# Column transforms moved between the last channels' products, and a PSUM tile for each step of the last channel, in a spectral block with a feed-forward network on one Trainium2 core

## The chip, the cores and the metric

The kernel runs on one core of one Trainium2 chip. The metric is the time of one execution in microseconds (us) on the device; smaller is better. A core has a matrix engine (PE, or TensorE), a vector engine (DVE), a scalar engine (ACT), a general engine (POOL), and queues that issue DMA transfers (here SP's). Every engine runs its own instructions strictly in the order in which they were written; an instruction that needs another engine's result waits for a semaphore, and everything behind it on its engine waits too.

## The reference

```python
def _A_ref(x, w_r, w_i):                     # spectral mixing, S = 2048 rows, D = 576 columns
    X = rfft2(x.astype(float32), axes=(-2, -1))
    X = X * (w_r + 1j * w_i)
    return irfft2(X, s=(S, D), axes=(-2, -1)).astype(bfloat16)

def _B_ref(x, w_gate, w_up, w_down):         # D = 576, F = 4608
    return (_gelu(x @ w_gate) * (x @ w_up)) @ w_down

h = x + _A_ref(_layernorm(x), A_w_r, A_w_i)
h2 = h + _B_ref(_layernorm(h), B_w_gate, B_w_up, B_w_down)
```

x has 1 x 2048 x 576 values in bfloat16; the spectral weights have 2048 x 289, the feed-forward weights 576 x 4608 (twice) and 4608 x 576.

## The kernel before, in words

The whole first half, up to `h`, is a chain of small matrix products; the second half is the feed-forward network, four chunks of 512 rows.

**The spectral half.** The transform over the 2048 rows is split into 16 by 128. After the forward products the work runs over eight "channels" k, in the order `[1, 2, 3, 4, 5, 6, 7, 0]`, so the last channel is k = 0 and the one before it k = 7. The main loop is a pipeline written out by hand: in step i it issues

- `f2` (L449), the forward column transform of one channel: six products into a PSUM tile, and one copy to SBUF by ACT (L464) that makes the tile `pq`;
- `f3(k, half)` (L474), four products (L471 and L472) from `pq[k]` and `pq[k+8]` into a PSUM tile `gh_ps`, and a cast by ACT. For the ordinary channels the casts make `g` and `hs` (L492). For k = 0 they make `xab` directly (L483), and the first two of the four products need only `pq[0]`, the others `pq[8]`;
- `wmul` (L504), the multiplication with the spectral weights on DVE (L519 to L531), which writes the tile `Zt`. For the last channel it is done in two parts of columns, so `Zt` becomes ready in two halves;
- `i3(k, s)` (L535), the inverse products of channel k in three steps s. Each step writes a PSUM tile `eo_ps` that ACT, or DVE in one case, copies into `EO[x]`. An ordinary channel has ten products (L547 and L549). The last channel has eight products (L570) in each of its three steps. In the kernel before, steps 0 and 1 of every channel share one PSUM tile; for the last channel the copy of step 0 (ACT, L578) reads the tile's first half and that of step 1 (DVE, L578) its second half. Step 2 is copied by ACT at L583, and for ordinary channels at L556, steps 0 and 1 together at L551.

`EO[0]` is complete after channel 4, `EO[1]` only after the last channel.

**Column transforms.** `inv_cols(x, g)` (L591) is the inverse column transform number g, 0 to 7, of half x, 0 or 1: six products (L596) into a PSUM tile `cs_ps`, and a copy out by ACT. For g = 0 and 1 these are two copies into `cs` (L619; for half 1 the second of the two goes to DVE, L617), for larger g one copy into `cw` (L609). In the kernel before, transforms (0,0), (0,1), (0,2) stand between the products of channels 6 and 7, then come channel 7, the last channel, transform (0,3), and, after the weight pools have been set up, (1,0) and (1,1).

**Row products and the head of the feed-forward.** `add_rows(0)` and `add_rows(1)` (L708, tile `y_ps`) finish the rows of blocks h = 0 to 3. DVE adds them to `h_sb` (`add_sum`, L753), ACT sums the squares (L757), and `head_rstd` makes the statistics. Blocks 0 and 1 are normalised by DVE (`norm2`, L733, tile `hrow`) and turned by a DMA transpose on SP's queue (`flip`, L745); blocks 2 and 3 are normalised into `hflat` (L141) and turned by PE (`turn`, L778), copied by ACT and DVE (L779). In between, PE does the transforms that are left: (0,4) to (0,7) and (1,2) to (1,6), and (1,7) behind the turns. The feed-forward's first product (L845) needs all four blocks in `Bt`.

**The feed-forward.** For each chunk of 512 rows, 36 blocks of 18 products (L845), a Gelu on ACT (L853) and a product on DVE (L854), then the products with `w_down` (L865). Two thirds of `w_down` are loaded by `load_wd` (L673) on SP's queue; the first of these loads goes into memory that the spectral tiles free, so it waits for the last channel's products.

**What sets the order.** The schedule is manual: instructions stand on each engine in the order of the calls. From the middle of the kernel all PSUM tiles come from one pool of four buffers (`two`, two banks each). A new tile takes the buffer whose former tile was finished with longest ago in the written order, and its first product waits for the copy that read that former tile.

Of the kernel before, what the change touches and what calls it, by code (L numbers as in the profile page):

```python
# [20 lines left out]
P = 128  # L21
# [11 lines left out]
NJT = 3  # L33
# [8 lines left out]
def kernel_body(  # L42
# [24 lines left out]
    def two(name):  # L67
        return psum.tile([P, 2, 512], FP32, name=name, tag="two", bufs=3)
# [312 lines left out]
    def twiddles():  # L381
        sine_rows()
        A.activation(TF[:, :, 1, :], ab[:], ACT.Sin, bias=nhpib[:], scale=2.0 * PI / S)
        nc.sync.dma_start(
            TI[:].rearrange("p k r q -> p (k r) q"), TF[:].rearrange("p k r q -> p (k r q)"), transpose=True
        )
        nc.sync.dma_start(wd_a[:], wd_view[:, 0:NWA, :])

    def sine_rows():


        for dst, src in (
            (DI[64:128, :, 1, :], DT[0:64, 0, :, 1, :]),
            (DS[0:64, 0, :, :], DT[64:128, 0, :, 1, :]),
            (DS[64:128, 0, :, :], DT[0:64, 1, :, 1, :]),
            (DS[0:64, 1, :, :], DT[64:128, 1, :, 1, :]),
            (DS[64:128, 1, :, :], D3[0:64, :, 1, :]),
        ):
            nc.sync.dma_start(dst, src)
# [43 lines left out]
    order = [1, 2, 3, 4, 5, 6, 7, 0]  # L443
# [5 lines left out]
    def f2(c):  # L449
        ps = two("pq_ps")  # L450
        if c == 1:
            fill(ps[:, 0, :], 4)
        col = slice(slot[c] * P, (slot[c] + 1) * P)
        for par in range(2):
            for t in (par, par + 2, 4):
                T.matmul(  # L456
                    ps[:, par, 0:JP],
                    lhsT=Bt[:, t, col],
                    rhs=DT[:, t // 2, par] if t < 4 else DF[:, par],
                    start=(t == par),  # L460
                    stop=(t == 4),
                )
        sb = wk.tile([P, 2, JP], BF16, name="pq", tag="pq", bufs=6)
        (V.tensor_copy if c == 9 else A.copy)(  # L464
            sb[:].rearrange("p r (j a) -> p r j a", a=2),
            ps[:, :, 0:JP].rearrange("p a (r j) -> p r j a", r=2),
        )
        pq[c] = sb
# [29 lines left out]
    def sums_of(k):  # L498
        g, hs = gk[k], hk[k]
        x = xab[k] = wk.tile([P, 2, 2, JP], BF16, name="xab", tag="xab", bufs=2)  # L500
        V.tensor_tensor(x[:, 0, :, 0:J], g[:, :, 0:J], hs[:, :, 0:J], ALU.subtract)  # L501
        V.tensor_tensor(x[:, 1, ::-1, 0:J], g[:, :, 0:J], hs[:, :, 0:J], ALU.add)  # L502
# [32 lines left out]
    def i3(k, s):  # L535


        x, i = place[k]
        z = zt[k][:].rearrange("p c j -> p (c j)")
        if s != 1:  # L540
            eo[k] = two("eo_ps")
        ps = eo[k]
        if k:
            pv = ps[:].rearrange("p a (n h e l) -> p (a n) e h l", n=2, h=H, l=8)
            for n, w in (((0, 0), (1, 1)), ((2, 3), (3, 4)), ((0, 2),))[s]:
                o = w * P
                T.matmul(pv[:, n], lhsT=z[:, o : o + P], rhs=TI[:, k, 1:3, :], start=True, stop=False)  # L547
                o += 2 * ZS
                T.matmul(pv[:, n], lhsT=z[:, o : o + P], rhs=TI[:, k, 0:2, :], start=False, stop=True)  # L549
            if s == 1:  # L550
                A.copy(  # L551
                    EO[x][:, 0:4, :, :, i, :].rearrange("p w h e l -> p w (h e) l"),
                    ps[:].rearrange("p a (n r l) -> p (a n) r l", n=2, l=8),
                )
            elif s == 2:
                A.copy(  # L556
                    EO[x][:, 4, :, :, i, :].rearrange("p h e l -> p (h e) l"),
                    ps[:, 0, 0 : 2 * P].rearrange("p (r l) -> p r l", l=8),
                )
            return  # L560

        pv = ps[:].rearrange("p a (n h b l) -> p (a n) b h l", n=2, h=H, l=8)
        for n, c, j, p0, m in (
            ((0, 0, 0, 0, P), (1, 0, P, 0, P)),
            ((2, 1, 64, 0, P), (3, 1, 192, 0, P)),
            ((0, 0, 256, 0, 64), (0, 1, 0, 64, 64)),
        )[s]:
            for b in range(2):
                for a in range(2):
                    T.matmul(  # L570
                        pv[p0 : p0 + m, n, b],
                        lhsT=z[:, (2 * a + b) * ZS + j : (2 * a + b) * ZS + j + m],
                        rhs=TI[:, 8 * b, 1 - a + c, :],
                        start=(a == 0),
                        stop=(a == 1),
                    )
        if s < 2:
            (V.tensor_copy if s else A.copy)(  # L578
                EO[x][:, 2 * s : 2 * s + 2, :, :, i, :].rearrange("p w h e l -> p w (h e) l"),
                ps[:, s].rearrange("p (n r l) -> p n r l", n=2, l=8),  # L580
            )
        else:
            A.copy(  # L583
                EO[x][:, 4, :, :, i, :].rearrange("p h e l -> p (h e) l"),
                ps[:, 0, 0 : 2 * P].rearrange("p (r l) -> p r l", l=8),
            )
# [4 lines left out]
    def inv_cols(x, g):  # L591

        ps = two("cs_ps")
        for e in range(2):
            for jt in range(NJT):
                T.matmul(  # L596
                    ps[:, e, 0:JP],
                    lhsT=EO[x][:, 2 * e + jt if jt < 2 else 4, 2 * g : 2 * g + 2].rearrange("p h e k l -> p (h e k l)"),
                    rhs=DI[:, :, e, :] if jt == 2 else DS[:, jt] if e else DT[:, jt, :, 0, :],
                    start=(jt == 0),  # L600
                    stop=(jt == NJT - 1),
                )
        pv = ps[:, :, 0:JP].rearrange("p t (q a) -> p t q a", q=2)
        if g >= 2:
            if x == 0 or g == 2:
                cw[x, g] = eop.tile([P, 2, JP], FP32, name=f"cw{x}{g}")[:]
            else:
                cw[x, g] = cwb[:, g - 3]
            A.activation(  # L609
                cw[x, g].rearrange("p t (a q) -> p t q a", q=2), pv, ACT.Copy, scale=Y_SCALE  # L610
            )
            return
        ts = [eop.tile([P, JP], BF16, name=f"cs{x}{g}{t}") for t in range(2)]
        for t in range(2):
            dst = ts[t][:].rearrange("p (a q) -> p q a", q=2)
            if x == 1 and t == 1:
                V.tensor_scalar(dst, pv[:, t], Y_SCALE, None, op0=ALU.mult)  # L617
            else:
                A.activation(dst, pv[:, t], ACT.Copy, scale=Y_SCALE)  # L619
        cs[x, g] = ts  # L620
# [3 lines left out]
    n = len(order)  # L624
    for i in range(n + 1):
        last = i >= n
        if not last:
            f2(order[i])
        if i == 0:
            twiddles()  # L630
        if 1 <= i <= n:
            f3(order[i - 1], 0)
        if i >= 3 and not last:
            i3(order[i - 3], 0)
        if 1 <= i <= n:
            f3(order[i - 1], 1)
            if i == 1:
                sums_of(order[0])
            else:
                wmul(order[i - 2], i - 1, order[i - 1])  # L640
        if i >= 3 and not last:
            i3(order[i - 3], 1)
        if not last:
            f2(order[i] + 8)
        if i == 0:
            weights()
        if i >= 3:
            for jt in range(0 if last else 2, NJT):
                i3(order[i - 3], jt)
        if last:  # L650
            wmul(order[i - 1], i)
        if i == 1:
            late_tables()
            scr_pool.__exit__(None, None, None)
            eop = ctx.enter_context(tc.tile_pool(name="eop", bufs=1, side="right"))
            EO = [eop.tile([P, 5, H, 2, 4, 8], BF16, name=f"EO{x}", tag=f"EO{x}") for x in range(2)]
    for g in range(3):
        inv_cols(0, g)
    for k in order[6:]:
        for jt in range(NJT):  # L660
            i3(k, jt)
    inv_cols(0, 3)

    spw.__exit__(None, None, None)
    spec.__exit__(None, None, None)
# [118 lines left out]
    def norm_row(h):  # L784
        hrow = ln2[h] = roll.tile([P, D], BF16, name="hflat", tag="hrow", bufs=4)
        normalise(V, hrow[:], mv2, rstd2, h)
# [4 lines left out]
    y1 = add_rows(1)  # L791
    add_sum(0, y0)
    add_sum(1, y0)
    inv_cols(0, 4)
    add_sum(2, y1)
    head_rstd(0)
    add_sum(3, y1)
    head_rstd(1)
    inv_cols(0, 5)
    norm2(0)  # L800
    flip(0)
    head_rstd(2)
    inv_cols(0, 6)
    head_rstd(3)
    norm2(1)
    flip(1)
    inv_cols(0, 7)
    inv_cols(1, 2)
    norm_row(2)
    norm_row(3)  # L810
    for g in range(3, 7):
# [20 lines left out]
    for tcnk in range(4):  # L832
        for gi in range(NG):
            fa = gi * FQ
            w = groups.pop(0)
            n = tcnk * NG + gi + 2
# [21 lines left out]
        for st in range(4):  # L858
            h = tcnk * 4 + st
            last = h == H - 1  # L860
# [70 lines left out]
```

## Time and profile before

| | |
|---|---|
| median of 3 runs | 510.33 us (510.31 to 510.36) |
| profiled execution, its own time | 510.62 us |
| span of the profiled execution | 508.4 us |
| PE busy | 494.4 us (97%) |
| PE weight loads busy | 287.0 us (56%) |
| DVE busy | 214.7 us (42%) |
| ACT busy | 152.4 us (30%) |
| granted PE clock | 1.0 |
| feed-forward's first product | at 79.8 us of the span |

The span runs from the first to the last instruction; the execution's own time is 2.2 us longer. Products on PE overlap: a row of the timeline gives the start and the length of one, and the next may start before it ends. In the timeline a bracket at the end of a row is the idle time of that engine before it, and the engine, tile and line that ended it. In the chain of waits each row is a piece of the chain that ended last, with its start and length. The waits are inferred from semaphore events.

### The profile page before, as it was taken

The page shows a single profiled execution, that of the slowest core. Times are in us where ns is not written, and L with a number is a line of the kernel's source. Part 1 is how long each engine was busy: PE and PEld are TensorE (multiplying, and loading weights), DVE is VectorE, ACT ScalarE, POOL GpSimd, SP SyncE. Part 2 cuts the span into 40 slices and gives each one's busy share as a digit, 9 for nine tenths or more (in the row PEclk, how much of TensorE's full clock was granted, in tenths as well). Part 3 has the DMA queues.
Part 4 walks back from the last instruction along what each step waited for, and adds up shares of the span by engine and source line. Part 5 has one row for each costly group of instructions (what it writes and reads, how often), then busy time and mean ns, then how long its engine had stood idle before and what let it go on. Part 6 is the DMA issues. An engine that isn't in the chain of part 4 may idle for free.

```text
span 508.4 us, 9921 instructions
## 1 busy us (share of the span) xinstructions
PE 494.4 (97%) x4353; PEld 287.0 (56%) x4355; DVE 214.7 (42%) x418; ACT 152.4 (30%) x265; POOL 32.6 (6%) x81
## 2 busy tenths in 40 slices
PE   6889999999999999999999999999999999999997
PEld 2457765444447774444467744444578544444775
DVE  8979964689662015433311034433201233333001
ACT  7688975233220003323210023232200132323000
POOL 8700010111110000000000000000000000000000
PEclk9999999999999999999999999999999999999999
DMA  8985057779970009998730089978500487770000
GB/s 285 230 151 154 1 153 203 148 145 198 198 148 3 0 24 206 184 202 157 143 69 0 1 175 198 189 158 159 104 0 1 115 161 159 160 153 3 13 12 25
DMA packets 86811, 60.85 MB, mean 120 GB/s; under 512 B 22640, under 2 KB 85488, under 8 KB 86768
## 3 DMA queue, kind: packets, MB, share of 16 engines
q1 hardware_dynamic: 86480, 59.03, 57.8%
q0 software_dynamic: 288, 1.18, 0.9%
q8 instruction: 34, 0.56, 0.5%
q14 instruction: 9, 0.07, 0.1%
HBM read 52.65 MB, written 2.36 MB: 108 GB/s over the span
## 4 chain that ended last, share of the span: by engine, by line
PE 90%; DVE 7%; ACT 1%; DMA 1%; issue 0%; POOL 0%; DVEq 0%; ACTq 0%
PE gu L845 55%; PE acc L865 28%; DVE m L519 2%; PE cs_ps L596 2%; PE f2t L261 2%; PE y_ps L708 1%; DVE za L525 1%; DMA h_sb<-in_A_x_dram 1%; PE f2t L249 1%; DVE xab L502 1%; PE f L270 1%; DVE Zt L530 1%; DVE zb L526 1%; DVE Zt L531 1%; DVE xab L501 0%
## 5 line engine op out<-in xcount | busy, mean ns | idle before, releaser
L845 PE MATMUL gu<-Bt,wgu 64*128 64x512 bf16 x2592 | 281.4, 376 | 0.0
L845 PEld LDWEIGHTS <-wgu 64*128 64x128 bf16 x2592 | 125.8, 94 | 152.5 <-issue 0.7
L853 ACT ACTIVATE g_sb<-gu 128x512 f32<-128x512 f32 x144 | 86.0, 597 | 301.9 <-PE gu L845 301.8
L854 DVE TENSOR_TENSOR P_sb<-g_sb,gu 128x512 bf16<-128x512 f32 x144 | 98.7, 685 | 151.8 <-ACT g_sb L853 151.8
L865 PEld LDWEIGHTS <-P_sb 128*128 128x128 bf16 x1152 | 112.4, 98 | 30.6 <-issue 2.4
L865 PE MATMUL acc<-wd,P_sb 128*128 128x288 bf16 x768 | 99.3, 286 | 0.0
L877 DVE TENSOR_TENSOR h_sb<-h_sb,acc 128x576 bf16<-128x576 bf16 x15 | 11.3, 754 | 118.2 <-PE acc L865 118.2
L865 PE MATMUL acc<-wd_a,P_sb 128*128 128x288 bf16 x384 | 52.3, 286 | 0.5 <-DVE h_sb L873 0.5
L249 PE MATMUL f2t<-h_sb,ident 128*128 128x512 bf16 x39 | 11.9, 434 | 4.4 <-DMA h_sb<-in_A_x_dram 4.4
L456 PE MATMUL pq_ps<-DT,Bt 128*128 128x290 bf16 x64 | 12.4, 287 | 0.0
L733 DVE TENSOR_SCALAR hrow<-h_sb,mv,rstd 128x1152 bf16<-128x1152 bf16 x14 | 12.1, 867 | 0.0
L138 POOL TENSOR_TENSOR rstd<-rstd,mhalf 128x1 f32<-128x1 f32 (+2 forms) x17 | 11.8, 693 | 1.4
L249 PEld LDWEIGHTS <-ident 128*128 128x128 bf16 x45 | 4.8, 107 | 11.5 <-issue 5.2
L261 PE MATMUL f2t<-F,xn 128*128 128x256 bf16 x64 | 9.7, 274 | 1.6 <-DVE xn L141 1.5
L137 POOL TENSOR_SCALAR rstd<-mv 128x1 f32<-128x1 f32 (+2 forms) x17 | 4.0, 237 | 110.1 <-DVE mv L122 109.9
L596 PEld LDWEIGHTS <-EO 128*128 128x128 bf16 x96 | 9.0, 96 | 3.0 <-issue 0.2
L456 PEld LDWEIGHTS <-Bt 128*128 128x128 bf16 x96 | 9.2, 97 | 2.5
L464 ACT CAST pq<-pq_ps 128x580 bf16<-128x580 f32 x15 | 9.9, 662 | 0.9 <-PE pq_ps L456 0.8
L120 DVE BATCH_NORM_STATS2 st<-h_sb 128x6 f32<-128x288 bf16 x22 | 9.8, 444 | 0.0
L121 DVE BATCH_NORM_STATS2 st<-h_sb 128x6 f32<-128x288 bf16 x22 | 9.7, 442 | 0.0
L471 PE MATMUL gh_ps<-pq,TF 128*128 128x289 bf16 x32 | 8.6, 286 | 1.1 <-ACT pq L464 0.6
L280 ACT CAST Bt<-f2t 128x1024 bf16<-128x1024 f32 x8 | 8.1, 1011 | 4.4 <-PE f2t L261 4.4
(135 smaller groups left out, 263.1 us busy)
## 6 DMA issues: line engine op xcount, KB each, us to landing
wgu<-in_B_w_gate_dram SPq DMA_DIRECT2D x48, 432.0 KB, 5.2
wgu<-in_B_w_up_dram SPq DMA_DIRECT2D x48, 432.0 KB, 6.7
wd<-in_B_w_down_dram SPq DMA_DIRECT2D x2, 1728.0 KB, 8.1
h_sb<-in_A_x_dram SPq DMA_DIRECT2D x3, 576.0 KB, 6.5
wd_a<-in_B_w_down_dram SPq DMA_DIRECT2D x1, 1728.0 KB, 9.0
out_dram<-h_sb SPq DMA_DIRECT2D x3, 576.0 KB, 3.4
WR<-in_A_w_r_dram SPq DMA_DIRECT2D x1, 650.2 KB
WI<-in_A_w_i_dram SPq DMA_DIRECT2D x1, 650.2 KB, 13.4
```

Source lines behind the costliest of these rows:

```text
L138: G.tensor_tensor(dst[:, sl], dst[:, sl], mhalf[:, sl], ALU.pow)
L249: T.matmul(dst, lhsT=ident[:], rhs=h_sb[:, 2, 0:512], start=True, stop=True)
L261: T.matmul(f2t[:, h % 2, t * 2 * P : (t + 1) * 2 * P], lhsT=x[:, d0 : d0 + P], rhs=F16[:, n : n + 2, :], start=(n == 0), stop=(n == 1),)
L456: T.matmul(ps[:, par, 0:JP], lhsT=Bt[:, t, col], rhs=DT[:, t // 2, par] if t < 4 else DF[:, par], start=(t == par), stop=(t == 4),)
L519: V.tensor_tensor(m[:, :, :, js], x[:, :, :, js], w[:, sl, js].unsqueeze(1).to_broadcast([P, 2, 2, j1 - j0]), ALU.mult,)
L596: T.matmul(ps[:, e, 0:JP], lhsT=EO[x][:, 2 * e + jt if jt < 2 else 4, 2 * g : 2 * g + 2].rearrange("p h e k l -> p (h e k l)"), rhs=DI[:, ...
L733: V.tensor_scalar(hrow[:], h_sb[:, h, :].rearrange("p (r k) -> p r k", k=64).unsqueeze(2).to_broadcast([P, NR, 2, 64]), mv2[:, h, 0:1], rs ...
L845: T.matmul(gu[:, c, :], lhsT=w[rows, r, i * P : (i + 1) * P], rhs=hl[tcnk % 2][rows, r, :], start=(r == 0), stop=(r == NR - 1),)
L853: A.activation(g_sb[:], gu[:, 0, :], ACT.Gelu_apprx_tanh)
L854: V.tensor_tensor(p_sb(fa + i), g_sb[:], gu[:, 1, :], ALU.mult)
L865: T.matmul(acc[:, c, 0:DH], lhsT=p_sb(f)[:, st * P : (st + 1) * P], rhs=wd[f // NWA][:, f % NWA, cc], start=(f == 0), stop=(f == NFT - 1),)
L877: V.tensor_tensor(hv, hv, acc[:, :, 0:DH], ALU.add)
```

## The change

Four edits, all in the spectral half and the head of the feed-forward. No instruction is added or removed on any compute engine or DMA queue; the instructions stand in another order, and the last channel's tiles are others.

1. `i3` for k = 0 takes a PSUM tile of its own in each of the three steps; step 1 writes into the first half of its own tile.
2. Transform (0,0) goes from behind channel 6's products to the place ahead of the last channel's `f3`.
3. Behind channel 6 stand (0,1) and (0,2), as before; between channel 7 and the last channel stand (0,3) and (0,4) where there were none; behind the last channel stands (0,5) instead of (0,3).
4. Of the transforms behind the row products, (0,6) and (0,7) move up, and (1,2) takes a place ahead of the statistics of block 3; seven transforms are left ahead of the turns where there were nine.

```diff
@@ i3 @@
-        if s != 1:
+        if s != 1 or k == 0:
             eo[k] = two("eo_ps")
...
             ((0, 0, 0, 0, P), (1, 0, P, 0, P)),
-            ((2, 1, 64, 0, P), (3, 1, 192, 0, P)),
+            ((0, 1, 64, 0, P), (1, 1, 192, 0, P)),
             ((0, 0, 256, 0, 64), (0, 1, 0, 64, 64)),
...
-                ps[:, s].rearrange("p (n r l) -> p n r l", n=2, l=8),
+                ps[:, 0].rearrange("p (n r l) -> p n r l", n=2, l=8),
@@ the loop over channels @@
         if i == 0:
             twiddles()
+        if last:
+            inv_cols(0, 0)
         if 1 <= i <= n:
             f3(order[i - 1], 0)
@@ behind the loop @@
-    for g in range(3):
+    for g in (1, 2):
         inv_cols(0, g)
-    for k in order[6:]:
-        for jt in range(NJT):
-            i3(k, jt)
-    inv_cols(0, 3)
+    for s in range(3):
+        i3(order[6], s)
+    for g in (3, 4):
+        inv_cols(0, g)
+    for s in range(3):
+        i3(order[7], s)
+    inv_cols(0, 5)
@@ behind the row products @@
-    inv_cols(0, 4)
+    inv_cols(0, 6)
     add_sum(2, y1)
     head_rstd(0)
     add_sum(3, y1)
     head_rstd(1)
-    inv_cols(0, 5)
+    inv_cols(0, 7)
     norm2(0)
     flip(0)
     head_rstd(2)
-    inv_cols(0, 6)
+    inv_cols(1, 2)
     head_rstd(3)
     norm2(1)
     flip(1)
-    inv_cols(0, 7)
-    inv_cols(1, 2)
```

## The prediction, made before the changed kernel was run

> **What bounds the kernel now.** I read the page first, for the span and for groups that wait for nothing.
>
> ```profile
> span 508.4 us, 9921 instructions
> ...
> L845 PE MATMUL gu<-Bt,wgu 64*128 64x512 bf16 x2592 | 281.4, 376 | 0.0
> ```
>
> The feed-forward products had no idle time in front of them (the 0.0 at the end). So the change cannot shorten that stretch, only let it begin earlier or later. I therefore read the chain of waits that leads up to its first product.
>
> ```profile
> 64.86 0.59 ACT EO L578
> 65.46 0.04 issue
> 65.50 0.96 PE eo_ps L570 x16
> 66.46 2.35 PE cs_ps L596 x18
> 68.81 2.26 PE y_ps L708 x32
> 71.07 6.84 PE cs_ps L596 x54
> 77.91 1.13 PE pt L778 x36
> 79.03 0.85 PE cs_ps L596 x6
> ```
>
> From 65.50 us on, PE is the chain: the last channel's products (L570), three column transforms, the row products (L708), nine more transforms, the transposes, one transform. A transform costs 6.84/9 = 0.76 us, a product of it 0.13. The one link here that is not PE is ACT's copy L578 of step 0: step 1 writes into the same PSUM tile and waits for it. The timeline of PE alone shows the holes.
>
> ```profile
> 57.32 0.29 PE L472 MATMUL gh_ps<-pq,TF 128*128 128x289 bf16 x1
> 58.21 0.28 PE L471 MATMUL gh_ps<-pq,TF 128*128 128x289 bf16 x1 [0.60 <-ACT pq L464]
> ...
> 62.28 0.27 PE L547 MATMUL eo_ps<-TI,Zt 128*128 128x256 bf16 x1
> ...
> 63.37 0.39 PE L570 MATMUL eo_ps<-TI,Zt 128*128 128x128 bf16 x4
> 64.25 0.58 PE L570 MATMUL eo_ps<-TI,Zt 128*128 128x128 bf16 x4 [0.50 <-DVE Zt L525]
> 65.50 0.96 PE L570 MATMUL eo_ps<-TI,Zt 128*128 128x128 bf16 x16 [0.67 <-ACT EO L578]
> 66.39 0.42 PE L596 MATMUL cs_ps<-DT,EO 128*128 128x290 bf16 x2
> ```
>
> The first column is the start, the bracket the idle time and who ended it. Products overlap, so I count from start to start. After 57.32 the next product could have started 0.13 later: the hole is 58.21 - 57.45 = 0.76 us. Products of L570 start every (66.39 - 65.50)/16 = 0.056 us: four of them fill 63.37 to 63.59, and the second hole is 64.25 - 63.59 = 0.66 us. The third is the wait for L578, 0.67 us.
>
> **The change, part by part.** *Transform (0,0) ahead of the last channel's f3.* It enters where the first of the two products before the hole began, 57.32 - 0.13 = 57.19. It needs a free PSUM tile; in the order as built this is the one that the cast of hs (L492) frees, two ACT instructions ahead of the cast at 57.49 below. It ends at 57.95, the two products that need only pq[0] at 58.21, and the next one could not start before 58.21 in any case. On PE it costs nothing, because the hole covers it; without the hole it would cost 0.76. What it lengthens is ACT's queue, where its two copies (L619) come ahead of the casts of xab (L483).
>
> ```profile
> 57.49 0.66 ACT L464 CAST pq<-pq_ps 128x580 bf16<-128x580 f32 x1
> 58.03 0.41 ACT L556 CAST EO<-eo_ps 128x256 bf16<-128x256 f32 x1
> 58.65 1.19 ACT L483 CAST xab<-gh_ps 128x578 bf16<-128x578 f32 x2 [0.22 <-PE gh_ps L472]
> 60.02 1.01 ACT L551 CAST EO<-eo_ps 128x1024 bf16<-128x1024 f32 x1 [0.18 <-PE eo_ps L549]
> 60.93 0.38 ACT L556 CAST EO<-eo_ps 128x256 bf16<-128x256 f32 x1
> 61.20 1.58 ACT L619 ACTIVATE cs<-cs_ps 128x290 bf16<-128x290 f32 x4
> 62.55 0.78 ACT L609 ACTIVATE cw<-cs_ps 128x580 f32<-128x580 f32 x1
> ```
>
> One copy is 1.58/4 = 0.40 us. The two run from 58.4 to 59.2, and the casts of xab end at 60.4, where they ended at 59.84. DVE's L519 of the last channel waits for them, behind this instruction:
>
> ```profile
> 61.29 0.46 DVE L531 TENSOR_TENSOR Zt<-zb,za 128x578 bf16<-128x578 bf16 x1
> ```
>
> DVE is busy until 61.75, so 1.3 us of slack remain and the last channel's Zt is as early as before.
>
> *Two transforms instead of three, then channel 7.* Its products started at 62.28; one transform less, they could start at 61.52, but half of them need the Zt that ends at 61.75. They take 63.37 - 62.28 = 1.09 us, to 62.85. *Transforms (0,3) and (0,4), then the last channel.* 2 x 0.76 gives 64.35. The second half of the last Zt let products go at 64.25, so the 0.66 us hole is filled by transforms and the last channel meets data that is ready. Its PSUM tiles must be free too, which is ACT's work: the casts of channel 6 (L551, L556), three copies of L619's and L609's kind and channel 7's L551 take ACT from 60.4 to 1.01 + 0.38 + 0.79 + 0.78 + 1.01 = 64.35 by full durations, and to 63.8 if they overlap as rows do start to start (L551 0.91, L556 0.27). That is level with PE or ahead.
>
> *A PSUM tile for each step.* Steps 0, 1 and 2 run without the wait for L578: 24 x 0.056 = 1.35 us, to 65.7. Next late is ACT: behind L551 stand L556, two copies of 0.78, L578 and a last copy as large as L556: 0.38 + 1.56 + 0.59 + 0.38 = 2.9 us, ending at 66.3 to 67.2. Transform (1,0) needs the last of these at its third product, 65.7 + 0.76 + 0.25 = 66.7. So here 0 to 0.5 us may be lost.
>
> *The sum to y_ps.* The three transforms before y_ps started at 66.39 and start at 65.7: 0.69 us earlier. With the loss on ACT's side it could be 0.2. I take 0.7, since on most of these meetings ACT is ahead and its rows do overlap.
>
> *Behind y_ps* stand two transforms fewer, so PE could reach the feed-forward another 2 x 0.76 = 1.52 us earlier. But the first product also waits for two DMA transposes of rows 0 and 1 (L745), issued when DVE has normalised them (L733). The answers for the tile Bt, for DVE, for PE's queue and for PE:
>
> ```profile
> L745 SPq DMA_TRANSPOSE Bt<-hrow x2: 1261/1277/1293, 74.3 to 75.9; - x2
> ...
> DMA to landing us min/median/max: 3.6/3.6/3.6
> ```
>
> ```profile
> 74.99 0.86 DVE L733 TENSOR_SCALAR hrow<-h_sb,mv,rstd 128x1152 bf16<-128x1152 bf16 x1
> ```
>
> ```profile
> 78.57 1.16 DVE L779 COPY Bt<-pt 128x1152 bf16<-128x1152 bf16 x2 [2.04 <-PE pt L778]
> ```
>
> ```profile
> L845 PEldq EVENT_SEMAPHORE  x1: 51/51/51, 79.5 to 79.5; - x1
> ```
>
> ```profile
> 79.82 9.89 PE L845 MATMUL gu<-Bt,wgu 64*128 64x512 bf16 x90
> ```
>
> The second transpose is issued at 75.9, when L733 ends (74.99 + 0.86), and lands 3.6 us later, at 79.5. PE's queue passed its wait for it at 79.5; the first product, held by DVE's copy L779 until 79.73, began at 79.82. DVE's instructions between y_ps and L733 keep their order, so this landing moves with y_ps alone, to 78.8. PE is there at about 77.8, idles 1.1 us and starts some 0.1 us after the landing, at 78.9. Of the 1.52 us there remain 0.2, by which the landing was ahead of the copy's end.
>
> *Sum.* 0.7 + 0.2 = 0.9 us: span 508.4 to 507.5, the profiled execution's 510.62 to 509.72. The median of the runs shown, 510.33, is 0.29 below that execution; the same gain on it gives 509.4 us.
>
> *A rule on idle PE.* PE was slow once in this trace:
>
> ```profile
> L249 PE MATMUL f2t<-h_sb,ident x9: 448/634/634, 4.4 to 7.8; 128*128 128x512 bf16 x9
> ```
>
> Nine products of 512 columns started 3.4/8 = 0.43 us apart; L845's pairs of that width start 9.89/45 = 0.22 apart. After the 0.76 us hole the products took 0.28 us as before it, so such a hole does no harm; one of 1.1 us is not in the rows shown. The Trainium skill (TensorE: Matmul & The Clock Gate, Part 1) says that the clock halves only after an idle window of about 3.4 us. By that rule the sum stands.
>
> **The rivals.** *A, the transposes don't hold it.* If they land earlier than I read, PE's order decides: 0.7 + 1.52, less some 0.25 where PE then waits for ACT's copies, 2.0 us, 508.3. Against it: landing and passed wait agree on 79.5. Chance 0.10.
>
> *B, ACT becomes the bound before y_ps.* Transform (1,0) waits 0.4 to 0.5 us; y_ps gains 0.25, the total is 0.45, 509.9. For it: ACT had hardly a hole between 57.49 and 63.3. Against it: only one meeting is short. Chance 0.12.
>
> *C, slower: the transposes meet the load of wd* (L673), which goes ahead of them on SP's queue.
>
> ```profile
> 66.62 0.37 SPq L673 DMA_DIRECT2D wd<-in_B_w_down_dram  x1
> ```
>
> ```profile
> wd<-in_B_w_down_dram SPq DMA_DIRECT2D x2, 1728.0 KB, 8.1
> ...
> Bt<-hrow SPq DMA_TRANSPOSE x14, 6.9
> ```
>
> 66.62 + 8.1 = 74.7: it ends about when the first transpose is issued, 74.3. All 14 transposes have a median of 6.9 us, these two 3.6. If they slip to 6.9, everything starts 3.3 us later: 509.4 + 3.3 = 512.7. It decides from where the load ends over 1 us after that first issue. Against it: the load waits for the last channel's products, which move earlier by as much as y_ps. The Trainium skill (Trainium Kernel Development and Optimization, Key Constraints) says that all queues run on the same 16 DMA engines and interleave; this rival would need that. Chance 0.10.
>
> *D, the longer idle time slows PE.* Half the rate for 3.4 us, as at 4.4 to 7.8, costs 1.7: 511.1. Chance 0.04.
>
> That the transforms don't move is excluded by the order as built; what can fail is that the holes close.
>
> **How the numbers follow.** About 0.2%, 1.0 us, is what a measurement of this kernel can tell from no change. My forecast, chance 0.64, gives 0.55 to 1.15 us of gain and so lies across that bound: 0.30 of it counts as faster, 0.34 as same. Faster: 0.30 + A 0.10 = 0.40. Same: 0.34 + B 0.12 + D 0.04 = 0.50. Slower: C 0.10. The range, 508.2 to 510.4, holds the forecast, A and B, and leaves out C and D, 0.14.
>
> **What would show it.** Right: no wait of PE for L578; a product L471 near 58.2 behind six of L596; y_ps near 68.1; about 1 us of PE idle before L845, ended by the transposes near 78.9. Wrong: that idle ends on DVE or ACT (A); y_ps after 68.4, with PE waiting for ACT (B); transposes over 4 us to landing (C); L845 rows over 376 ns behind it (D); or a cast of xab that ends after 61.7.

## The result, and the profile after

The changed kernel takes 509.33 us (median of 20 runs, 509.0 to 510.55), the kernel before 510.63 us beside it (20 runs, 510.31 to 512.04). The ratio is 0.9974 with a 95% interval of 0.9968 to 0.9981: about 1.3 us, or 0.26%, faster. The upper ends of these ranges come from a few runs of each kernel (two of the 20 after, three of the 20 before) that took over 1 us longer; where the clock of such runs is on record, it was granted at 0.996 to 0.997, against 0.998 to 1.0 in the others. The profiled execution took 509.37 us with a span of 507.2 us, against 510.62 and 508.4 before. In the changed file lines up to 630 keep their numbers or nearly so; L673 became L678, L708 L713, L733 L738, L745 L750, L753 L758, L778 L783, L779 L784, L845 L848, L865 L868 and L873 L876.

First the page of the changed kernel, its span and the group of the feed-forward's first products.

```profile
span 507.2 us, 9921 instructions
L848 PE MATMUL gu<-Bt,wgu 64*128 64x512 bf16 x2592 | 281.5, 376 | 0.9 <-DMA Bt<-hrow 0.9
```

The stretch itself has not changed: 2592 products, 376 ns each, 281.5 us busy against 281.4. New is 0.9 us of idle time ahead of it, ended by the DMA transposes. Now PE's timeline in the changed kernel, rows chosen at the three places where there were holes, at the start of channel 7, and at the feed-forward.

```profile
57.20 0.41 PE L596 MATMUL cs_ps<-DT,EO 128*128 128x290 bf16 x2
57.95 0.28 PE L471 MATMUL gh_ps<-pq,TF 128*128 128x289 bf16 x1
58.21 0.28 PE L471 MATMUL gh_ps<-pq,TF 128*128 128x289 bf16 x1
...
61.54 0.27 PE L547 MATMUL eo_ps<-TI,Zt 128*128 128x256 bf16 x1
61.80 0.28 PE L549 MATMUL eo_ps<-TI,Zt 128*128 128x256 bf16 x1
...
62.79 0.41 PE L596 MATMUL cs_ps<-DT,EO 128*128 128x290 bf16 x2
...
64.29 1.41 PE L570 MATMUL eo_ps<-TI,Zt 128*128 128x128 bf16 x24
65.63 0.42 PE L596 MATMUL cs_ps<-DT,EO 128*128 128x290 bf16 x2
...
78.67 9.89 PE L848 MATMUL gu<-Bt,wgu 64*128 64x512 bf16 x90 [0.89 <-DMA Bt<-hrow]
```

Only the last row has a bracket. Transform (0,0) stands from 57.20 to 57.95, and the product of line 471 that needs the second half still starts at 58.21. The last channel's 24 products are one row, 64.29 to 65.63, where they were three rows with 0.50 and 0.67 us of waiting. One short wait is left: channel 7's second product starts 0.26 us behind its first, where products of this kind start 0.11 us apart. Last, the chain of waits of the changed kernel from there to the feed-forward.

```profile
65.69 2.34 PE cs_ps L596 x18
68.04 1.19 PE y_ps L713 x16
69.23 2.11 DVE h_sb L758 x6
...
72.77 0.78 DVE hrow L738
...
75.11 3.42 DMA Bt<-hrow
```

Before, this chain ran on PE alone from 65.50 us to the first feed-forward product at 79.82. Now it leaves PE at the row products, goes through the sums, the statistics and the normalising, most of them on DVE, and the transpose on SP's queue, and comes back to PE at 78.67. (The row of L738 here is the normalising of block 0; that of block 1, which the second transpose needs, runs on DVE from 74.22 to 75.08, as a row further down shows.) The feed-forward starts 1.15 us earlier. The rest is unchanged work: the tail behind the last output's issue is 507.2 - 504.60 = 2.60 us, against 508.4 - 505.74 = 2.66 before, the same within the rounding of the spans.

### The profile page after: what moved, and what is told of

Read it like the earlier page. It is cut to its first block, busy times and chain, and to the rows that moved or that the text cites. A ratio compares the mean times of both kernels' runs of the same rounds, so it can differ in the third digit from the quotient of the medians.

```text
span 507.2 us, 9921 instructions
## 1 busy us (share of the span) xinstructions
PE 494.9 (98%) x4355; PEld 292.4 (58%) x4355; DVE 214.7 (42%) x418; ACT 152.0 (30%) x265; POOL 32.6 (6%) x81
## 4 chain that ended last, share of the span: by engine, by line
PE 93%; DVE 4%; DMA 1%; ACT 1%; POOL 0%; issue 0%; ACTq 0%
PE gu L848 55%; PE acc L868 28%; PE f2t L261 2%; PE pq_ps L456 1%; PE cs_ps L596 1%; PE eo_ps L549 1%; PE y_ps L713 1%; PE eo_ps L547 1%; PE gh_ps L472 1%; PE f2t L249 1%; DMA Bt<-hrow 1%; PE gh_ps L471 1%; DMA h_sb<-in_A_x_dram 1%; PE f L270 1%; DVE h_sb L758 1%; DVE st L121 0%
## 5 line engine op out<-in xcount | busy, mean ns | idle before, releaser
L848 PE MATMUL gu<-Bt,wgu 64*128 64x512 bf16 x2592 | 281.5, 376 | 0.9 <-DMA Bt<-hrow 0.9
L848 PEld LDWEIGHTS <-wgu 64*128 64x128 bf16 x2592 | 130.9, 94 | 148.3 <-issue 1.9
L868 PEld LDWEIGHTS <-P_sb 128*128 128x128 bf16 x1152 | 112.4, 98 | 30.6 <-issue 2.4
L868 PE MATMUL acc<-wd,P_sb 128*128 128x288 bf16 x768 | 99.3, 286 | 0.0
L868 PE MATMUL acc<-wd_a,P_sb 128*128 128x288 bf16 x384 | 52.3, 286 | 0.5 <-DVE h_sb L876 0.5
L249 PE MATMUL f2t<-h_sb,ident 128*128 128x512 bf16 x41 | 13.2, 447 | 4.4 <-DMA h_sb<-in_A_x_dram 4.4
L738 DVE TENSOR_SCALAR hrow<-h_sb,mv,rstd 128x1152 bf16<-128x1152 bf16 x14 | 12.1, 866 | 0.0
L596 PE MATMUL cs_ps<-DI,EO 128*128 128x290 bf16 x32 | 9.1, 285 | 0.0
```

What stands on the lines that cost most here:

```text
L249: T.matmul(dst, lhsT=ident[:], rhs=h_sb[:, 2, 0:512], start=True, stop=True)
L596: T.matmul(ps[:, e, 0:JP], lhsT=EO[x][:, 2 * e + jt if jt < 2 else 4, 2 * g : 2 * g + 2].rearrange("p h e k l -> p (h e k l)"), rhs=DI[:, ...
L738: V.tensor_scalar(hrow[:], h_sb[:, h, :].rearrange("p (r k) -> p r k", k=64).unsqueeze(2).to_broadcast([P, NR, 2, 64]), mv2[:, h, 0:1], rs ...
L848: T.matmul(gu[:, c, :], lhsT=w[rows, r, i * P : (i + 1) * P], rhs=hl[tcnk % 2][rows, r, :], start=(r == 0), stop=(r == NR - 1),)
L868: T.matmul(acc[:, c, 0:DH], lhsT=p_sb(f)[:, st * P : (st + 1) * P], rhs=wd[f // NWA][:, f % NWA, cc], start=(f == 0), stop=(f == NFT - 1),)
```

## The experiments

The theory, T, is the prediction's mechanism: two savings lie one behind the other (the closed holes and the missing wait for L578 bring the row products forward; PE then gets ahead of the second transpose's landing, and that landing, not PE, sets the start of the feed-forward). The rivals to it are given with each run. Every kernel was timed beside the kernel before.

**The PSUM tile alone.** The kernel before with edit 1 only:

```diff
-        if s != 1:
+        if s != 1 or k == 0:
...
-            ((2, 1, 64, 0, P), (3, 1, 192, 0, P)),
+            ((0, 1, 64, 0, P), (1, 1, 192, 0, P)),
...
-                ps[:, s].rearrange("p (n r l) -> p n r l", n=2, l=8),
+                ps[:, 0].rearrange("p (n r l) -> p n r l", n=2, l=8),
```

> The kernel before with the first edit alone: a PSUM tile for each step of the last channel, every transform at its old place. Theory T (the wait for L578 was the link that set y_ps; behind y_ps the two DMA transposes set the start of the feed-forward): Zt's second half still lets products go at 64.25 us, 20 products of L570 and three transforms follow without a wait, y_ps starts near 67.9 (68.74 before, 67.97 after), and the feed-forward near 78.9, where PE and DVE's copy L779 are late, not the transposes: about 0.9 us less than before, 0.25 more than after. Rival R1 (the gain comes from the transforms that fill the holes): 0 to 0.3 us less than before.

Measured: 509.67 us (509.37 to 509.71) beside 510.61; ratio 0.9981, 95% 0.9972 to 0.9990. PE's timeline in this kernel:

```profile
64.23 1.38 PE L570 MATMUL eo_ps<-TI,Zt 128*128 128x128 bf16 x20 [0.48 <-DVE Zt L525]
...
67.89 2.33 PE L708 MATMUL y_ps<-cs,G 64*128 64x288 bf16 x32
...
78.96 1.25 PE L845 MATMUL gu<-Bt,wgu 64*128 64x512 bf16 x10
```

The wait for Zt is still there (0.48), the wait for L578 is gone, and the row products start 0.85 us earlier than before. All of that arrives: the feed-forward's first product moves from 79.82 to 78.96, and its row has no bracket, so PE did not wait for the transposes here. This small edit alone is worth 0.94 us, nearly three quarters of the whole, so rival R1 falls.

**The order alone.** The changed kernel with the shared PSUM tile put back (the diff above in reverse):

> The changed kernel without the first edit: the transforms at their new places, steps 0 and 1 of the last channel in one PSUM tile. Theory T: the wait for L578 is back and longer, since two copies of transforms stand ahead of L578 on ACT (it ends near 65.7); step 1 starts near 65.8, y_ps near 69.0, the transposes land near 79.6, the feed-forward starts at 79.7 to 79.8: 0 to 0.15 us less than before. Rival R1 (the filled holes are the gain): 0.7 us or more less than before, most of the change's gain.

Measured: 510.46 us (510.42 to 510.63); ratio 0.9998, 95% 0.9989 to 1.0007, no difference that can be measured. Its PE timeline:

```profile
64.28 0.61 PE L570 MATMUL eo_ps<-TI,Zt 128*128 128x128 bf16 x8
65.75 0.96 PE L570 MATMUL eo_ps<-TI,Zt 128*128 128x128 bf16 x16 [0.85 <-ACT EO L578]
...
68.98 2.32 PE L713 MATMUL y_ps<-cs,G 64*128 64x288 bf16 x32
...
79.66 0.61 PE L848 MATMUL gu<-Bt,wgu 64*128 64x512 bf16 x4 [0.87 <-DMA Bt<-hrow]
```

And one row of ACT in it:

```profile
63.95 1.28 ACT L609 ACTIVATE cw<-cs_ps 128x580 f32<-128x580 f32 x2
```

The hole ahead of the last channel is closed, but the wait for L578 behind it grew from 0.67 to 0.85 us, because ACT has the copies of transforms (0,3) and (0,4) ahead of L578, up to 63.95 + 1.28 = 65.23. The row products come later than before (68.98 against 68.74), and what the two transforms fewer behind them could have saved ends in the 0.87 us wait for the transposes. The two parts alone give 0.94 + 0.15 = 1.09 us, together 1.30. The intervals are too wide to call this difference shown; in the profiles the feed-forward starts 0.86 and 0.16 us earlier with one part alone and 1.15 with both, which points the same way.

**The transform in the first hole, put back.** The changed kernel with (0,0) behind channel 6 again:

```diff
-        if last:
-            inv_cols(0, 0)
...
-    for g in (1, 2):
+    for g in (0, 1, 2):
         inv_cols(0, g)
```

> The changed kernel with one thing put back: the column transform of channel 0's pair (0,0) stands behind channel 6's products again, as before, instead of in the hole that TensorE has ahead of the forward products of line 471. Theory T (the hole is idle time that ends on a fixed event, so a transform put into it is free and one taken out of it is paid in full behind it): channel 7 at about 62.28 us instead of 61.54, the last channel's products at 64.87 instead of 64.29, the first product of the second half (y_ps) at about 68.55 instead of 67.97, the first feed-forward product at about 79.25 instead of 78.67, and the time 0.58 us above the changed kernel's, 0.6 to 0.75 below the kernel before. Rival H (the 0.66 us wait ahead of the last channel takes the transform in as well, and the place of (0,0) makes no difference): y_ps at 67.97 and the time within 0.15 us of the changed kernel's.

Measured: 509.87 us (509.56 to 510.09), beside 510.62; ratio 0.9980, 95% 0.9971 to 0.9988. That is 0.54 us above the changed kernel run with it (509.33, 509.04 to 509.35, 7 runs). PE's timeline of this kernel, then the same rows of the changed kernel's second profile:

```profile
64.55 1.41 PE L570 MATMUL eo_ps<-TI,Zt 128*128 128x128 bf16 x24
...
68.24 1.98 PE L711 MATMUL y_ps<-cs,G 64*128 64x288 bf16 x27
...
79.14 2.12 PE L846 MATMUL gu<-Bt,wgu 64*128 64x512 bf16 x18 [1.09 <-DMA Bt<-hrow]
```

```profile
64.00 1.41 PE L570 MATMUL eo_ps<-TI,Zt 128*128 128x128 bf16 x24
...
67.69 2.32 PE L713 MATMUL y_ps<-cs,G 64*128 64x288 bf16 x32
...
78.34 2.98 PE L848 MATMUL gu<-Bt,wgu 64*128 64x512 bf16 x26 [0.85 <-ACT cwb L609]
```

These two are compared with each other because both executions began 0.3 us ahead of the other profiles (see the end). The row products are 0.55 us later without the transform in the hole, T's 0.58. It is not the transform's whole 0.76 us, because the changed kernel's channel 7 waits for its Zt (the 0.26 us between 61.54 and 61.80 above, 0.15 more than between its other products), and this wait takes in part of the transform. Rival H, that the later hole would take the transform in as well, falls. In this profile the feed-forward is 0.80 us later and not 0.55, since its second transpose took 3.6 us to land, against 3.4; the medians show 0.54. The last row of the second fence names ACT's copy L609, which there ended in the moment in which the transpose landed (78.2). It is not what the feed-forward waits for: in a kernel below it starts ahead of that copy's end.

**Does the second transpose hold the feed-forward?** Two runs. In the first, block 1 of the changed kernel is turned by PE instead of by a DMA transpose, which adds 18 products to PE:

```diff
-        parts = ((V.tensor_copy, 0, NR),) if h == 2 else ((A.copy, 0, 4), (V.tensor_copy, 4, NR))
+        parts = ((V.tensor_copy, 0, NR),) if h < 3 else ((A.copy, 0, 4), (V.tensor_copy, 4, NR))
...
-    norm2(1)
-    flip(1)
+    norm_row(1)
...
+    turn(1)
```

> The changed kernel, but block 1 is normalised into hflat and turned by PE ahead of blocks 2 and 3, with one copy by DVE, instead of by the second DMA transpose. Theory T (after the change PE idles 0.9 us because the second transpose lands at 78.5): the one transpose left lands near 77.0 and holds nothing; PE has 18 transposes more, 0.57 us, no idle time, and the feed-forward starts near 78.3 where it started at 78.67: 0.3 to 0.4 us less than the changed kernel, 1.5 to 1.6 less than before. Rival R2 (PE's own order sets that start, the landing only coincides): 0.5 to 0.6 us more than the changed kernel.

Measured: 509.22 us (508.92 to 510.65); ratio 0.9975, 95% 0.9965 to 0.9984. PE's timeline:

```profile
75.58 1.76 PE L783 MATMUL pt<-ident,hflat 128*64 128x128 bf16 x54
...
78.12 2.12 PE L848 MATMUL gu<-Bt,wgu 64*128 64x512 bf16 x18
```

The wait is gone: although PE does 0.56 us more work, it starts the feed-forward at 78.12, 0.55 us earlier than the changed kernel. So the transpose did hold it, and rival R2 falls. But the median fell by only 0.11 us, where 0.3 to 0.4 were expected. The last output was issued at 504.04, 0.56 us earlier, and the span ended at 507.1, 3.06 us behind it. A second run of the same kernel, with the changed kernel itself beside it, asked whether this comes again:

> The kernel with block 1 turned by TensorE again, unchanged, to see whether what it gave back behind the last output's issue comes again. Its last output transfer was issued at 504.04 us, 0.56 us earlier than in the changed kernel, but its span ended at 507.1 us, 3.06 us behind that issue and not 2.6. If the longer tail belongs to this schedule, the span is 507.1 again, the tail 3.0 to 3.1 us, and the median 0.1 us below that of the changed kernel run beside it; if it was chance of one execution, the tail is 2.6 to 2.7 us in this profile and the median 0.5 us below the changed kernel's.

> The changed kernel itself on the chip and in the rounds of the two others, as their neighbour: T and its rivals alike expect 509.3 us, 1.2 to 1.3 us below the kernel before, y_ps at 68.0 us, the second transposing transfer landed 3.3 to 3.6 us behind its start, and the first feed-forward product at 78.6 to 78.9 us.

Measured: 509.22 us again (508.92 to 510.55) against 509.33 for the changed kernel; last issue at 503.72, span 506.8, a tail of 3.08 us, where the changed kernel has 506.9 - 504.26 = 2.64. So the longer tail comes again with this schedule. The trace shows where it is: at the kernel's closing waits on SP's queue (L929). First three of these waits in the changed kernel, from the one that the last output's landing ends, then the same three in the first profile with block 1 turned by PE (in the second they stand from 505.3 to 505.8).

```profile
L929 SPq EVENT_SEMAPHORE  x3: 28/28/28, 506.2 to 506.3; - x3
```

```profile
L929 SPq EVENT_SEMAPHORE  x3: 28/28/28, 505.6 to 506.1; - x3
```

The landing is passed 1.6 us behind the output's issue in both kernels (504.60 to 506.2, 504.04 to 505.6). Behind it the three waits take 0.1 us in the first kernel and 0.5 us in the second, which is most of the 0.4 us by which the tail is longer. What holds SP there is not shown. It is not the transfer of instruction code that comes later in the second kernel (at about 506.7 us, in the first at 506.1): it begins behind these waits and takes 0.45 us, so it was still running when the span ended at 507.1. The cause of the longer tail stays open.

In the second run, DVE normalises block 1, and its transpose is issued, ahead of the statistics of blocks 2 and 3, so that the second transpose may start as soon as the queue is through with the first:

```diff
+    norm2(1)
+    flip(1)
     head_rstd(2)
     inv_cols(1, 2)
     head_rstd(3)
-    norm2(1)
-    flip(1)
```

> The changed kernel with norm2(1) and flip(1) put ahead of the statistics of blocks 2 and 3 on DVE. Theory T: the second transpose is issued as soon as SP is done with the first, 73.58 + 1.29 = 74.87 instead of 75.11, lands 0.24 us earlier, and the feed-forward starts as much earlier, near 78.45, although blocks 2 and 3 are normalised up to 0.5 us later. Rival R2: the feed-forward starts 0 to 0.5 us later than in the changed kernel, because PE waits for hflat longer.

Measured: 509.26 us (508.97 to 510.86); ratio 0.9977, 95% 0.9968 to 0.9986. The answer for the tile Bt and PE's timeline:

```profile
L750 SPq DMA_TRANSPOSE Bt<-hrow x2: 1287/1290/1292, 73.6 to 75.0; - x2
...
DMA to landing us min/median/max: 3.3/3.3/3.3
```

```profile
78.43 1.90 PE L848 MATMUL gu<-Bt,wgu 64*128 64x512 bf16 x16 [0.60 <-DMA Bt<-hrow]
```

ACT's timeline in the same kernel:

```profile
77.87 0.68 ACT L609 ACTIVATE cwb<-cs_ps 128x580 f32<-128x580 f32 x1 [0.54 <-PE cs_ps L596]
```

The start moves with the landing, from 78.67 to 78.43 as T said, although ACT's copy L609 of the last transform ended only at 77.87 + 0.68 = 78.55 here. More was not to be had at this place, because the queue itself needs 1.29 us for the first transpose before it starts the second. Of this 0.24 us the span shows 0.2 (507.0 against 507.2), the profiled execution's own time 0.12 (509.25 against 509.37) and the median 0.07; where the rest goes is not shown. The intervals of these last two kernels overlap with that of the changed kernel, so neither is a proven improvement on it.

No run moves transforms (0,3) and (0,4), or the transforms of edit 4, by themselves: what each place is worth alone is shown for (0,0) only.

## Why the prediction was right, and what it mis-sized

The forecast was 509.4 us and the measurement 509.33, within the range. The gain was 1.3 us, though, and not 0.9. The prediction took its median from three runs (510.33). Of the 20 runs beside the changed kernel seven lie near 510.33 and ten near 510.64, so that the median is 510.63; with 0.9 us that base would have given 509.7. Part of the agreement is luck, then, and 0.4 us of the gain was missed: 0.25 us at the start of the feed-forward (1.15 against 0.9), and 0.15 us that no row shows: the start and the last output's issue (505.74 to 504.60) moved by 1.15, the profiled execution's own time by 1.25 and the median by 1.30. Point by point:

- *Transform (0,0) costs nothing in the hole*: right. It ran from 57.20 to 57.95 (said: 57.19 to 57.95), the second pair at 58.21 (58.21), and putting it back cost 0.54 us. That is less than the 0.76 us that the prediction names as its cost without the hole, since channel 7's wait for Zt takes in part of it.
- *Channel 7 and the transforms (0,3), (0,4)*: right. Transform (0,3) started at 62.79 (said 62.85), the last channel at 64.29 (64.35), without a wait.
- *A tile for each step*: right, and the largest part. The three transforms before the row products started at 65.63 (said 65.7). The 0 to 0.5 us that ACT might have cost there did not show: the last of ACT's copies there (L583) ended at 66.12, where the prediction had 66.3 to 67.2 (its own terms, 63.8 + 2.9, give 66.7 for the lower end). So rival B fell: y_ps came 0.77 us earlier where 0.7 was said.
- *The second transpose holds the feed-forward*: right in kind, but one term was too large. PE idled 0.9 us (1.1 had been said) and the wait was ended by the transposes, as foretold, so rival A (PE's order decides, 2.0 us) fell. But the term "lands 3.6 us later" was taken over from before; in the changed kernel the two transposes took 3.4 us. The answers for the tile Bt and for DVE in the changed kernel:

```profile
L750 SPq DMA_TRANSPOSE Bt<-hrow x2: 1261/1276/1292, 73.6 to 75.1; - x2
...
DMA to landing us min/median/max: 3.4/3.4/3.4
```

```profile
74.22 0.86 DVE L738 TENSOR_SCALAR hrow<-h_sb,mv,rstd 128x1152 bf16<-128x1152 bf16 x1
```

  The normalising of block 1 came 0.77 us earlier (74.22 against 74.99), just as y_ps did; then 0.2 us less to the landing. With 0.2 us by which the landing was ahead of DVE's copy before, this makes the 1.15 us, but for rounding: 0.07 + 0.2 are the mis-sized terms of the start. Landing in 3.4 us was also seen with the PSUM tile alone and 3.3 with the early normalising, 3.5 to 3.6 with (0,0) put back: a spread of 0.3 us within which the prediction took the upper end. What sets it is not shown.
- *Rival C, the transposes meet the load of wd*: fell, since they landed sooner and not in 6.9 us. *Rival D, the idle time slows PE*: fell. Behind 0.9 us without a product the first 90 products took 9.89 us, as they did before, and the granted clock was 1.0. This agrees with the Trainium skill (TensorE: Matmul & The Clock Gate, Part 1), by which only an idle window of about 3.4 us halves the clock. Less can do it, though: in the first profile with block 1 turned by PE the last product ended at 502.75 + 0.78 = 503.53 us, and the granted clock was 1.00 up to 506.0 and 0.50 from 506.1 on, some 2.5 us later. The 0.9 us here are well below both.
- *The chances*: 0.40 for faster by over 0.2% and 0.50 for no change put the larger weight on the wrong side of the bound, as a gain of 0.9 us lies just short of it (1.0 us) and one of 1.3 us beyond it.

## What to carry to other kernels

Read holes from start to start on the bounding engine and ask what event ends each: a hole that ends on a fixed event takes in other work for nothing, and work taken out of it is paid for, less what the next hole takes in (0.55 of 0.76 us here). When two steps share a tile and two engines read its halves, the second step waits for the first step's reader; a tile for each step was worth more here than the whole reordering, and the reordering alone gave nothing that could be measured, because its gain ran into exactly that wait. After each gain on one engine, follow the chain again up to the next start: here it passed from PE to a transposing transfer, and the last 0.55 us gained at that start came back as only 0.1 us at the end.

## What the runs showed that was not expected

Most times of the kernel before and of the changed kernel fall on two levels about 0.3 us apart (near 510.33 and 510.63, and near 509.02 and 509.33). The two profiles of the changed kernel, of 509.37 and 509.04 us, happen to show one of each. The first column transform's products in the first and in the second:

```profile
30.65 0.41 PE L456 MATMUL pq_ps<-DT,Bt 128*128 128x290 bf16 x2
```

```profile
30.37 0.41 PE L456 MATMUL pq_ps<-DT,Bt 128*128 128x290 bf16 x2
```

The 0.28 us is there at 30 us of the span already, long ahead of anything that the change touches, and stays to the end (spans 507.2 and 506.9). What causes it is not shown. A median of three runs can lie wholly on one level, as that of the kernel before did; with differences of 0.1 to 0.3 us one should compare profiles that began alike.
